# Cached attention decode: most K and V tile loads issued from GpSimd's software DMA queue, a DMA engine's eight rows as one packet

## The chip, the core and the metric

The kernel runs on one core of a Trainium2 chip. The core has TensorE (matrix products), VectorE, ScalarE, GpSimd and SyncE, each with its own instruction stream, and 16 DMA engines that move data between HBM and the on-chip memory SBUF. A DMA is issued from an engine's stream into a queue; the 16 DMA engines work through the queues. The metric is device microseconds of one execution, lower is better; where several runs are told, their median.

## The reference

Two independent sets of inputs, A and B, go through the same attention step with one query token per sequence; the two results stand side by side. Everything is bf16.

```python
def _A_ref(x, k_cache, v_cache, wq, wo):       # B=8, Sq=1, D=1024, H=32, Sk=4096, Dh=128
    q = (x @ wq).reshape(B, Sq, H, Dh).transpose(0, 2, 1, 3)
    scores = einsum("bhqd,bhkd->bhqk", q, k_cache) * (Dh ** -0.5)
    p = softmax(scores, axis=-1)
    o = einsum("bhqk,bhkd->bhqd", p, v_cache)
    return o.transpose(0, 2, 1, 3).reshape(B, Sq, H * Dh) @ wo
```

For each set the K cache and the V cache are 8 x 32 x 4096 x 128 values, and each is read once. Four caches of 268 MB and the weights make the 1107 MB that the profile counts.

## The kernel before

**Tiles.** One tile is eight heads of one sequence: 8 x 4096 x 128 values, 8.39 MB, laid on 128 partitions of 64 KB each, so that each of the 16 DMA engines moves eight rows of 64 KB. There are NQ = 64 K tiles and 64 V tiles (2 sets x 8 sequences x 4 groups of heads), written k0 to k63 and v0 to v63 here. Weights wq and wo of a set are each one tile of the same size. All tiles live in `ring`, three slots of SBUF (line 196): K tiles alternate between slots 0 and 1, V tiles use slot 2 (the last, v63, uses slot 0). A list, `plan` (line 271), has the order of loads: wq A, k0, wq B, k1, v0, k2, v1, k3, v2, and so on, with v63, wo A and wo B last. wo B is cut into four pieces.

**The work on one tile pair n.** A K tile is worked on in four chunks. VectorE multiplies a chunk by the query, broadcast over the partitions (`make_mul`, line 362), and adds its two halves of the head dimension (`make_fold`, line 367). TensorE adds up further by matmuls with an identity (`make_eacc`, line 377), and VectorE reduces the rest (`make_red`, line 385). After four chunks VectorE finds a shift (`make_shift`, lines 391 to 395), ScalarE takes the exponential (line 397), and VectorE spreads the weights over eight columns (`make_pm`, line 402). TensorE multiplies them by the V tile in two halves (`make_pv`, line 414); ScalarE copies the sum (line 422), TensorE extracts (line 431), ScalarE copies out (line 437). The query of the next tile is staged by ScalarE (line 344), broadcast by TensorE (line 349) and copied (line 351).

**The order.** The loop at line 498 writes the instructions of each engine in order. The V part of tile n-1 is put into the chunks of tile n: the shift and the spreading after its first chunk's multiplication, the first half of PV(n-1) in its third chunk, ahead of that chunk's identity matmuls, and the second half in its fourth chunk, ahead of that chunk's. The identity matmuls of a chunk run one chunk ahead of VectorE's reduction of it. After the main passage the last tile is finished, then come the normalisation (`make_norm`) and the projection by wo (`make_proj`, line 467).

**Loads.** `load_tiles` (line 291) issues the loads in the order of `plan`, each as soon as the last user of its slot is known. A K tile's slot is free when the fourth chunk's identity matmuls of its former tenant are done, a V tile's when the second half of PV is. All of these loads are issued from SyncE, by `load_cache` (line 235) for K and V and by `dma` (line 232) for the weights: one hardware queue, served in order. Each waits on a TensorE semaphore first. The small inputs x come from ScalarE's hardware queue at the start. GpSimd has only set-up work at the start (memsets and selects).

**Semaphores and loops.** A DMA into slot w raises the semaphore of key `("t", w)` by 16. The engines' streams are straight code with a loop in the middle: `_repeat` finds that every round waits for the same semaphores with counts that grow evenly. TensorE's loop starts at tile 1, VectorE's and ScalarE's at tile 3 (line 544). SyncE and GpSimd have straight code.

Of the kernel before, what the change touches and what calls it, by code (L numbers as in the profile page):

```python
# [51 lines left out]
class _Program:  # L52
# [13 lines left out]
    def add(self, eng, emit, deps=(), dma_key=None, moves=False):  # L66
        op = _Op(eng, emit, list(deps), dma_key, moves)
        if dma_key is not None:
            self.counts[dma_key] = self.counts.get(dma_key, 0) + 16
            op.token = (dma_key, self.counts[dma_key])  # L70
        for d in op.deps:
            if not (d.eng == "pe" and eng == "pe"):
                d.sig = True
        self.ops[eng].append(op)
        return op
# [89 lines left out]
def _build_kernel(nc, caches, out):  # L165
    B, Sq, D = caches[0][0].shape
    _, H, Sk, Dh = caches[0][1].shape
    NC = len(caches)
# [8 lines left out]
    HB = H // HQ  # L177
    NQ = NC * HB * B
# [3 lines left out]
    MB = HQ * PH  # L182
    NT = 4
    DT = D // NT

    es = ExitStack()
    with es:
# [8 lines left out]
        ring = sb("ring", [128, 3, T * Dh], BF16)  # L196
# [10 lines left out]
        pe = sb("pe", [128, T], BF16)  # L207
# [3 lines left out]
        on_sb = sb("on_sb", [128, NC, B * H + H], BF16)  # L211
        orow = sb("orow", [128, NC, DT], BF16)
        q_sb = PM[:].rearrange("p t j -> p (t j)").rearrange("p (c n) -> p c n", c=NC)
# [8 lines left out]

        wo_cuts = ((0, 20), (20, H - 4), (H - 4, H - 1), (H - 1, H))
        sems = {e: es.enter_context(nc.semaphore(f"c_{e}")) for e in ENGINES[1:]}
        for name, n in (("t", 3), ("w", len(wo_cuts)), ("x", 1), ("out", 1)):
            for i in range(n):
                sems[(name, i)] = es.enter_context(nc.semaphore(f"{name}{i}"))

        P = _Program()
        add = P.add  # L230

        def dma(out_ap, in_ap, key, deps, eng="sp"):
            return add(eng, lambda e: e.dma_start(out_ap, in_ap), deps, dma_key=key)

        def load_cache(to, n, side, key, deps):
            c = where(n)[0]
            size = HQ * Sk * Dh
            whole = caches[c][side].rearrange("b h s d -> (b h s d)")

            def emit(e, at):  # L240
                return e.dma_start(to, whole[bass.ds(at(n % (B * HB) * size, size), size)].rearrange("(p x) -> p x", p=128))
            return add("sp", emit, deps, dma_key=key, moves=True)


        def pool_select(view, base, pattern, dep, op=ALU.not_equal, fill=1.0, step=1):
# [38 lines left out]
        def where(n):  # L284

            return n // (B * HB), n // HB % B, n % HB
# [4 lines left out]
        def load_tiles():  # L291
            while issued[0] < len(plan):
                kind, n, w = plan[issued[0]]
                prev = before[issued[0]]
                dep = opUse.get(prev)
                if prev is not None and dep is None:
                    return
                to, key = ring[:, w, :], ("t", w)
                if kind in ("k", "v"):
                    opT[(kind, n)] = load_cache(to, n, 1 if kind == "k" else 2, key, [dep])  # L300
                elif kind == "wq":
                    opT[(kind, n)] = dma(to[:, 0:DC * H * Dh], caches[n][3].rearrange("(p k) n -> p (k n)", k=DC), key, [dep])
                else:
                    from_ = caches[n][4].rearrange("(p r) n -> p (r n)", r=H)
                    for i, (r0, r1) in enumerate(wo_cuts if n == NC - 1 else ((0, H),)):
                        opT[(kind, n, i)] = dma(to[:, r0 * D:r1 * D], from_[:, r0 * D:r1 * D], key if n < NC - 1 else ("w", i), [dep])
                issued[0] += 1
# [151 lines left out]
        def make_proj(c):  # L459
            w = tile_of("wo", c)  # L460

            for i, (r0, r1) in enumerate(wo_cuts if c == NC - 1 else ((0, H),)):
                def emit(e, r0=r0, r1=r1):
                    for r in range(r0, r1):
                        for q in range(NT):
                            col = r * D + q * DT
                            x = e.matmul(proj[32 * q:32 * (q + 1), 0:DT], on_sb[:, c, r:r + H * B:HQ],  # L467
                                         w[:, col:col + DT], start=(r == 0), stop=(r == H - 1), tile_position=(0, 32 * q))
                    return x
                opProj[c] = add("pe", emit, [opNorm[c], opT[("wo", c, i)], c_pad, opEv.get(c - 1)])  # L470
            if c == NC - 1:
                for engname in P.hinted:
                    add(engname, turn, [opT[("wo", c, len(wo_cuts) - 1)]])
            opEv[c] = add("dve", lambda e: e.tensor_copy(orow[:, c, :], proj[:, 0:DT]), [opProj[c]])  # L474
            outs.append(dma(out[:, 0, c * D:(c + 1) * D].rearrange("b (q n) -> q b n", q=NT), orow[0:128:32 // B, c, :],
# [6 lines left out]
        def emit_xT(e):  # L482
# [5 lines left out]
            return i  # L488
        op_xT = opUse[("x", 0)] = add("pe", emit_xT, [c_ident, op_x[-1]])
        load_tiles()  # L490
        c_xT = add("dve", lambda e: e.tensor_copy(xT[:], misc_bf16[:, 0:NC * DC * B]), [op_xT])
        make_q(0)
# [5 lines left out]
        for n in range(NQ):  # L498
            P.mark(n)
            for r in range(NR):  # L500
                s = n * NR + r
                make_mul(s)
                if s >= LAG:
                    make_red(s - LAG)
                if r == LAG - 1 and n >= 1:
                    make_shift(n - 1)
                fold = make_fold(s)
                if r == LAG - 1 and n >= 1:
                    make_pm(n - 1)
                if n == 0 and r == NR - 1:  # L510
                    for c in range(1, NC):
                        make_q(c)
                        make_qT(c)
                if r == 2 and n >= 1:
                    make_pv(n - 1, 0, RG // 2)
                if r == 3 and n >= 1:
                    make_pv(n - 1, RG // 2, RG)
                    make_acc(n - 1)
                if r == 2 and n + 1 < NQ:
                    make_stage(n + 1)  # L520
                    make_qbc(n + 1)
                make_eacc(s, fold)
                load_tiles()
                if r == 3 and n >= 1:
                    make_ext(n - 1)
        P.mark(NQ)
        n = NQ - 1
# [4 lines left out]
        make_pv(n, 0, RG)  # L532
        make_acc(n)
        load_tiles()
        make_ext(n)
        make_norm(1)
# [4 lines left out]
        counts = P.tokens()  # L541
        for o in op_x:
            o.token = (("x", 0), 16 * NC)
        loops = {"pe": [(1, 2, (NQ - 2) // 2)], "dve": [(3, 2, (NQ - 4) // 2)], "act": [(3, HB, (NQ - 4) // HB)]}

        P.run("sp", nc.sync, sems, part=(0, 2))
        with nc.Block() as block:
# [24 lines left out]
def bass_concat_heads__mha_block_cached__mha_block_cached__decode_kernel(  # L572
    nc, A_x, A_k_cache, A_v_cache, A_wq, A_wo, B_x, B_k_cache, B_v_cache, B_wq, B_wo, out,
):
    caches = [(A_x, A_k_cache, A_v_cache, A_wq, A_wo), (B_x, B_k_cache, B_v_cache, B_wq, B_wo)]
    _build_kernel(nc, caches, out)
# [28 lines left out]
```

## Time and profile before

| | |
|---|---|
| median of 3 runs | 2559.17 us (2559.16 to 2559.21) |
| profiled execution | 2559.26 us |
| its span, first to last instruction | 2558.0 us |
| mean granted TensorE clock | 0.687 |
| read from HBM | 1107.33 MB, 433 GB/s over the span |
| VectorE busy | 2170.2 us |
| TensorE busy | 1117.0 us |

The profile is one execution. Its time is 1.3 us more than its span. A group's line has the source line, the engine, the operation, what it writes and reads, how often, its busy time, the mean time of one in ns, and the idle time just before it with what ended that. A timeline's line has the start and the duration in microseconds, and in brackets the idle time before it and who ended it. `PE` is TensorE, `DVE` VectorE, `ACT` ScalarE, `POOL` GpSimd, `SP` SyncE, and a `q` behind an engine's name is its stream of issues. A queue's line has the number of packets, the MB and the time that its packets took, as a share of the 16 DMA engines' time; q1 is SyncE's hardware queue, q10 ScalarE's, and the kind "instruction" is the loading of code. "DMA packets" counts a tile's row of 64 KB as one packet, and each DMA engine's write of a semaphore as another of 4 bytes.

### The profile page before, as it was taken

How to read it: one execution, taken by the hardware profiler on the slowest of the kernel's cores; microseconds unless marked ns; L12 is line 12 of the kernel's file. 1: busy time of each engine (PE TensorE's matmuls, PEld its weight loads, DVE VectorE, ACT ScalarE, POOL GpSimd, SP SyncE). 2: the span in 40 equal slices, each digit the busy share in tenths (PEclk: the TensorE clock that was granted, in tenths of full speed). 3: DMA queues.
4: the chain of work that ended last, by engine and by line, in shares of the span. 5: the costliest groups of instructions: out<-in, count | busy, mean ns of one | idle time of the engine just before them, and what ended most of it. 6: DMA issues, size and time to landing. Idle time of an engine off the chain costs nothing.

```text
span 2558.0 us, 18889 instructions
## 1 busy us (share of the span) xinstructions
PE 1117.0 (44%) x7712; PEld 396.9 (16%) x7712; DVE 2170.2 (85%) x1042; ACT 129.9 (5%) x401; POOL 2.6 (0%) x15
## 2 busy tenths in 40 slices
PE   2443443443443444444444434444444434434435
PEld 0111111111111111111111111111111111111112
DVE  3898898898898898898898888988988988988983
ACT  1100000000000000000000000000000000000000
POOL 0000000000000000000000000000000000000000
PEclk8666676766767766766666767767767666666667
DMA  9999999999999999999999999999999999999999
GB/s 426 428 440 429 440 429 440 429 438 431 435 433 435 433 432 436 430 439 430 439 430 439 431 439 430 439 430 439 430 438 431 438 431 438 431 436 432 433 436 396
DMA packets 19552, 1107.49 MB, mean 433 GB/s; under 512 B 2184, under 2 KB 2248, under 8 KB 2520
## 3 DMA queue, kind: packets, MB, share of 16 engines
q1 hardware_dynamic: 19512, 1107.34, 99.9%
q8 instruction: 7, 0.11, 0.0%
q10 hardware_dynamic: 32, 0.03, 0.0%
q14 instruction: 1, 0.01, 0.0%
HBM read 1107.33 MB, written 0.03 MB: 433 GB/s over the span
## 4 chain that ended last, share of the span: by engine, by line
DMA 52%; DVE 28%; issue 16%; PE 4%; ACT 0%; another core or an unknown queue 0%; DVEq 0%; SPq 0%
DMA ring<-in_A_k_cache_dram 25%; DMA ring<-in_B_k_cache_dram 25%; DVE ring L362 10%; DVE ring L367 10%; PE red L377 4%; DVE s_sb L385 4%; DVE PM L402 3%; DMA ring<-in_B_wo_dram 2%; DVE rmax L391 1%; DVE rtmp L392 0%; ACT PM L323 0%; PE o L317 0%; DVEq L161 0%; DVE ngm L395 0%
## 5 line engine op out<-in xcount | busy, mean ns | idle before, releaser
L362 DVE TENSOR_TENSOR ring<-ring,qbc 128x8192 bf16<-128x8192 bf16 x256 | 1131.2, 4419 | 306.0 <-DMA ring<-in_A_k_cache_dram 154.9
L377 PE MATMUL red<-ring,ident 128*128 128x512 bf16 x2048 | 782.0, 551 | 1387.8 <-DVE ring L367 1387.8
L367 DVE TENSOR_TENSOR ring<-ring 128x4096 bf16<-128x4096 bf16 x256 | 581.5, 2271 | 0.0
L377 PEld LDWEIGHTS red<-ring,ident 128*128 128x128 bf16 x2048 | 239.3, 128 | 1838.9 <-DVE ring L367 1490.3
L385 DVE TENSOR_REDUCE s_sb<-red 128x64 f32<-128x1024 f32 x256 | 311.2, 1215 | 3.5 <-PE red L377 3.5
L414 PE MATMUL pv<-ring,PM 128*32 128x512 bf16 x4096 | 274.0, 415 | 4.7 <-DVE PM L402 4.7
L402 DVE TENSOR_TENSOR PM<-pe,own_h 128x2048 bf16<-128x2048 bf16 x64 | 146.2, 2284 | 0.7 <-ACT pe L397 0.7
L414 PEld LDWEIGHTS pv<-ring,PM 128*32 128x32 bf16 x4096 | 103.8, 104 | 188.0 <-issue 115.1
L351 ACT ACTIVATE qbc<-misc 128x128 bf16<-128x128 f32 x64 | 17.8, 278 | 1091.7 <-PE misc L349 1091.7
L397 ACT ACTIVATE pe<-s_sb,ngm 128x256 bf16<-128x256 f32 x64 | 32.5, 508 | 465.6 <-DVE ngm L395 465.6
L422 ACT ACTIVATE accS<-pv 128x512 bf16<-128x512 f32 x64 | 38.2, 597 | 352.8 <-PE pv L414 352.8
L431 PEld LDWEIGHTS o<-accS,E 128*32 128x32 bf16 x1024 | 31.2, 100 | 49.4 <-issue 48.2
L431 PE MATMUL o<-accS,E 128*32 128x32 bf16 x1024 | 38.0, 185 | 0.7 <-ACT accS L422 0.7
L437 ACT ACTIVATE o_sb<-o 32x32 f32 (+1 forms) x64 | 11.9, 186 | 449.8 <-PE o L431 441.9
L391 DVE TENSOR_REDUCE rmax<-s_sb 128x1 f32<-128x256 f32 x64 | 26.9, 420 | 2.2
L474 DVE CAST orow<-proj 128x256 bf16<-128x256 f32 x2 | 0.8, 424 | 26.8 <-PE proj L467 26.8
L337 DVE COPY qT<-misc 128x64 bf16<-128x64 bf16 x8 | 3.5, 434 | 18.6 <-PE misc L333 18.6
L344 ACT ACTIVATE qst<-qT 128x128 bf16 (+1 forms) x64 | 18.7, 292 | 1.9 <-DVE qT L337 1.9
L467 PE MATMUL proj<-ring,on_sb 128*32 128x256 bf16 x256 | 11.7, 354 | 16.1 <-DMA ring<-in_A_wo_dram 8.1
L392 DVE TENSOR_SCALAR rtmp<-half,rmax 128x32 f32<-128x32 f32 x64 | 15.4, 241 | 2.3
L395 DVE TRANSPOSE_TENSOR_REDUCE ngm<-rtmp 128x1 f32<-128x32 f32 x64 | 13.5, 211 | 2.2
L349 PE MATMUL misc<-ident,qst 128*128 128x128 bf16 x64 | 14.7, 230 | 0.9 <-ACT qst L344 0.9
(33 smaller groups left out, 65.3 us busy)
## 6 DMA issues: line engine op xcount, KB each, us to landing
ring<-in_B_wo_dram SPq DMA_DIRECT2D x1, 5120.0 KB, 32.9
ring<-in_B_wo_dram SPq DMA_DIRECT2D x1, 2048.0 KB, 37.3
ring<-in_B_wo_dram SPq DMA_DIRECT2D x1, 768.0 KB, 38.7
ring<-in_A_k_cache_dram SPq DMA_DIRECT2D x32, 39.8
ring<-in_A_v_cache_dram SPq DMA_DIRECT2D x32, 27.8
ring<-in_B_k_cache_dram SPq DMA_DIRECT2D x32, 39.7
ring<-in_B_v_cache_dram SPq DMA_DIRECT2D x32, 27.8
ring<-in_B_wo_dram SPq DMA_DIRECT2D x1, 256.0 KB, 38.8
```

The lines of the kernel that those rows point to most:

```text
L344: return e.activation(qst[:, n % 2, :].rearrange("p (j m) -> p j m", m=MP), from_.unsqueeze(2).to_broadcast([128, HQ, MP]), ACTF.Copy)
L351: opQbc[n] = add("act", lambda e: e.activation(qbc[:, n % 2, :], misc[:, 0:Dh], ACTF.Copy), [opQb[n], _at(opMul, NR * (n - 2) + NR - 1)])
L362: opMul[s] = add("dve", lambda e: e.tensor_tensor(v, v, qbc[:, n % 2, :].unsqueeze(1).to_broadcast([128, CT, Dh]), ALU.mult), [opT[("k", n ...
L367: return add("dve", lambda e: e.tensor_tensor(v[:, :, 0:64], v[:, :, 0:64], v[:, :, 64:128], ALU.add), [opMul[s]])
L377: i = e.matmul(dst, ident[:], v[:, g, :, j, :], start=(j == 0), stop=(j == 3))
L385: opRed[s] = add("dve", lambda e: e.tensor_reduce(s_sb[:, n % 2, r * CT:(r + 1) * CT], red_ps[s % 2][:, :].rearrange("p (t w) -> p t w", w ...
L391: m = add("dve", lambda e: e.tensor_reduce(rmax[:], s_sb[:, n % 2, :], AX.X, ALU.max), [opRed[NR * n + NR - 1]])
L397: opExp[n] = add("act", lambda e, at: e.activation(pe[:], s_sb[:, n % 2, :], ACTF.Exp, bias=ngm[:, n % 2:n % 2 + 1], scale=scale, accum_ou ...
L402: opPM[n] = add("dve", lambda e: e.tensor_tensor(PM[:], pe[:].unsqueeze(2).to_broadcast([128, T, HQ]), own_h[:].unsqueeze(1).to_broadcast( ...
L414: i = e.matmul(pv_ps[32 * q:32 * (q + 1), :], PM[:, t:t + 4, :].rearrange("p t j -> p (t j)"), v[:, t * Dh:(t + 4) * Dh], start=(g == 0), ...
L422: opAcc[n] = add("act", lambda e: e.activation(accS[:], pv_ps[:], ACTF.Copy), [opPV[n], _at(opExt, n - 1)])
L431: x = e.matmul(to, E[:, i, PH - 1 - u:PH - 1 - u + MB], accS[:, i * 128 + H * u:i * 128 + H * (u + 1)], start=(i == 0 and u == 0), stop=(i ...
```

## The change

```diff
+    HARD = {"k": 3, "v": 2}
...
-        for name, n in (("t", 3), ("w", len(wo_cuts)), ("x", 1), ("out", 1)):
+        for name, n in (("t", 3), ("g", 3), ("w", len(wo_cuts)), ("x", 1), ("out", 1)):
...
+            soft = key[0] == "g"
 
             def emit(e, at):
-                return e.dma_start(to, whole[bass.ds(at(n % (B * HB) * size, size), size)].rearrange("(p x) -> p x", p=128))
-            return add("sp", emit, deps, dma_key=key, moves=True)
+                from_ = whole[bass.ds(at(n % (B * HB) * size, size), size)].rearrange("(p x) -> p x", p=128)
+                return e.dma_start(to, from_, single_packet=True) if soft else e.dma_start(to, from_)
+            return add("pool" if soft else "sp", emit, deps, dma_key=key, moves=True)
...
-                to, key = ring[:, w, :], ("t", w)
+                to, key = ring[:, w, :], ("t" if n < HARD.get(kind, NC) else "g", w)
...
-        loops = {"pe": [(1, 2, (NQ - 2) // 2)], "dve": [(3, 2, (NQ - 4) // 2)], "act": [(3, HB, (NQ - 4) // HB)]}
+        loops = {"pe": [(3, 2, (NQ - 4) // 2)], "dve": [(3, 2, (NQ - 4) // 2)], "act": [(3, HB, (NQ - 4) // HB)]}
```

K tiles k3 to k63 and V tiles v2 to v63 are issued from GpSimd's stream into its software queue, whose descriptors (the DMA engines' orders) a program on GpSimd writes. The eight rows that a DMA engine moves for such a tile form one packet. The tiles before, and all weights, stay on SyncE's hardware queue. Software loads raise semaphores of their own, `("g", w)`, so that TensorE's waits change with the tiles; its loop starts at tile 3 instead of 1 and runs 30 rounds of two tiles instead of 31. What each load waits for, the slots and the order of `plan` are as before.

## Prediction

> **What bounds the kernel now.** First the page's shares, its queues and the chain of waits, then the transfers of the steady stretch.
>
> ```profile
> PE 1117.0 (44%) x7712; PEld 396.9 (16%) x7712; DVE 2170.2 (85%) x1042; ACT 129.9 (5%) x401; POOL 2.6 (0%) x15
> q1 hardware_dynamic: 19512, 1107.34, 99.9%
> DMA 52%; DVE 28%; issue 16%; PE 4%; ACT 0%; another core or an unknown queue 0%; DVEq 0%; SPq 0%
> ```
>
> One hardware queue carries all the data, and its packets fill the 16 DMA engines for 99.9% of the span. VectorE is the next engine at 85%. So a microsecond in which the engines have nothing to move is a microsecond of the result, and VectorE has some room. The DMA view of the stretch from the first tile's landing to the last K tile's:
>
> ```profile
> DMA packets 18148, 1057.03 MB, mean 434 GB/s; under 512 B 2016, under 2 KB 2016, under 8 KB 2016
> q1 hardware_dynamic: 18144, 1056.97, 100.2%
> q8 instruction: 3, 0.05, 0.0%
> ```
>
> The packets' times add up to 100.2% of the engines' time: they overlap slightly, and no idle time stands between rows. The timeline of VectorE shows when K tiles land (the multiplications that waited for a DMA):
>
> ```profile
> 81.86 4.43 DVE L362 TENSOR_TENSOR ring<-ring,qbc 128x8192 bf16<-128x8192 bf16 x1 [3.07 <-DMA ring<-in_A_k_cache_dram]
> ...
> 120.66 4.42 DVE L362 TENSOR_TENSOR ring<-ring,qbc 128x8192 bf16<-128x8192 bf16 x1 [4.88 <-DMA ring<-in_A_k_cache_dram]
> ...
> 159.39 4.43 DVE L362 TENSOR_TENSOR ring<-ring,qbc 128x8192 bf16<-128x8192 bf16 x1 [4.82 <-DMA ring<-in_A_k_cache_dram]
> ...
> 2477.57 4.42 DVE L362 TENSOR_TENSOR ring<-ring,qbc 128x8192 bf16<-128x8192 bf16 x1 [4.69 <-DMA ring<-in_B_k_cache_dram]
> ```
>
> From tile k1 (81.86) to k63 (2477.57) are 62 periods: 2395.71 / 62 = 38.64 us for a K and a V tile. A tile takes 19.32 us and one of an engine's 16 rows 2.415 us. VectorE idles some 4.8 us in each period. The issues on SP's queue, in order v1, k3, v2, k4, v3:
>
> ```profile
> 111.95 0.33 SPq L241 DMA_DIRECT2D ring<-in_A_v_cache_dram  x1
> 119.32 0.33 SPq L241 DMA_DIRECT2D ring<-in_A_k_cache_dram  x1
> 150.75 0.33 SPq L241 DMA_DIRECT2D ring<-in_A_v_cache_dram  x1
> 158.26 0.33 SPq L241 DMA_DIRECT2D ring<-in_A_k_cache_dram  x1
> 189.48 0.33 SPq L241 DMA_DIRECT2D ring<-in_A_v_cache_dram  x1
> ```
>
> v2 is issued at 150.75, and k3 ahead of it ends at 159.39: its margin is 8.64 us. k4, issued at 158.26, waits for all of v2, which ends at 159.39 + 19.32 = 178.7: a K tile's margin is 20.4 us. Whatever a software issue costs is free up to these margins.
>
> **The change part by part.** 61 K tiles (k3 to k63) and 62 V tiles (v2 to v63) leave SP's queue; wq, k0 to k2, v0, v1 and wo stay.
>
> *The moved issues.* GpSimd's own 15 instructions are its set-up at the start; after that it only waits and issues, in SP's old order and on the same TensorE semaphores. Nothing else stands behind its waits. What a software issue takes until bytes flow is not in the trace. The nearest row from below is SP's first issue, at 0.80 us, with the packets counted up to 1.8 and up to 2.6 us:
>
> ```profile
> 0.80 0.40 SPq L233 DMA_DIRECT2D ring<-in_A_wq_dram  x1
> ...
> DMA packets 0, 0.00 MB, mean 0 GB/s; under 512 B 0, under 2 KB 0, under 8 KB 0
> ...
> DMA packets 16, 1.05 MB, mean 403 GB/s; under 512 B 0, under 2 KB 0, under 8 KB 0
> L590 POOL MEMSET const-uint8-127<- 128x1 uint8 x1 | 0.1, 102 | 0.0
> ```
>
> So at least 1.0 us. From above: if each of the 128 rows cost GpSimd its smallest instruction (102 ns), 13.1 us. I take 2 us, close to SP's row, since writing a descriptor is no whole instruction. In the steady loop 2 us is hidden under 8.64 and costs nothing; without that cover each microsecond above costs 61 us.
>
> A rule speaks against this part: the Trainium skill ("SBUF — State Buffer", the section on who interferes with whom) says that GpSimd can't write descriptors while VectorE is in a mode that uses both port pairs, and that two-input operations take only the read side. By its first half an issue would wait for VectorE to pause; no run here shows it. It gets its own rival below.
>
> *The joining.* Seven packet boundaries in each of 123 tiles go: 861 per engine. The rows that price a boundary are the 4-byte semaphore packets of the x loads (the last row of the fences on the x loads below): 8 packets take 0.2% of 16 engines x 2.5 us, 10 ns each. As packets overlap, the saving lies between 0 and 10 ns, 0 to 8.6 us in all. Below nothing I bound it by a slow period, the one from 81.86 to 120.66: 0.16 us over the mean, x 61 = 9.8 us lost. I take 2 us gained (2.4 ns a boundary): the overlap already hides about 0.2% x 2415 = 4.8 of the 10 ns.
>
> The Trainium skill ("DMA: Bandwidth & Descriptors", why small descriptors are slow) puts a packet's fixed cost at about 3 cycles, beside one cycle for each 32 B, and calls joining worthwhile only for descriptors up to 256 B. Beside the 2048 cycles of a 64 KB row that is 0.15%; by it the gain would be an estimated 3 us (61 x 38.64 x 0.15% x 7/8), and the sum 2566.
>
> *The hand-over from SP's queue to GpSimd's.* This is the largest term. In one queue k3 stands behind v1. In two, the engines choose. The trace has one place with two filled queues: the x loads on ACT's queue beside wq and k0 on SP's. Issues and landing, then the x queue's packets in 7 to 9.5 us (the rows of one x) and in 9.5 to 12 us (their semaphores); the next two stretches of 2.5 us read the same for the other x:
>
> ```profile
> 2.49 0.59 ACTq L233 DMA_DIRECT2D ring<-in_A_x_dram  x1
> 3.12 0.28 ACTq L233 DMA_DIRECT2D ring<-in_B_x_dram  x1
> ...
> 15.87 1.11 PE L486 MATMUL misc<-ident,ring 8*128 8x8 bf16 x16 [15.87 <-DMA ring<-in_B_x_dram]
> ...
> 43.27 4.42 DVE L362 TENSOR_TENSOR ring<-ring,qbc 128x8192 bf16<-128x8192 bf16 x1 [9.76 <-DMA ring<-in_A_k_cache_dram]
> ```
>
> ```profile
> q10 hardware_dynamic: 8, 0.02, 1.7%
> ...
> q10 hardware_dynamic: 8, 0.00, 0.2%
> ```
>
> x landed by 15.87, not after k0 at 43.27: one small packet went in after each 2.4 us row of the other queue. Engines take turns packet by packet. Now a packet of k3 holds eight rows and a packet of v1 one. k2 lands at 120.66, and v1's rows begin. k3, issued at 119.32 + 2, goes in after a row or two of v1, whole. Both tiles together are done when they were before, 120.66 + 38.64 = 159.3; but v1, which landed near 140.0, is now the last of the two. (The Trainium skill, "DMA: Bandwidth & Descriptors", on queues and rings, says that an engine drains a whole packet before it switches; of joined packets no run here shows it, and without it v1 lands one row earlier, a rival below.) TensorE's rows that need v1 and what stands behind them on TensorE:
>
> ```profile
> 142.82 1.93 PE L414 MATMUL pv<-ring,PM 128*32 128x512 bf16 x32
> 144.68 0.23 PE L349 MATMUL misc<-ident,qst 128*128 128x128 bf16 x1
> 146.96 1.90 PE L377 MATMUL red<-ring,ident 128*128 128x512 bf16 x8 [2.05 <-DVE ring L367]
> 148.79 1.91 PE L414 MATMUL pv<-ring,PM 128*32 128x512 bf16 x32
> 154.63 3.60 PE L377 MATMUL red<-ring,ident 128*128 128x512 bf16 x8 [3.93 <-DVE ring L367]
> ...
> 181.55 3.03 PE L414 MATMUL pv<-ring,PM 128*32 128x512 bf16 x32
> ```
>
> The first half of PV(1), at 142.82 before, starts at 159.3. Behind it stand the query broadcast (0.23), the third chunk's fold sums (line 377) and the second half; only then is v2 issued. That is 1.93 + 0.2 + 1.90 + 1.91 = 5.9 us with these fast rows, 3.03 + 0.2 + 3.60 + 3.03 = 9.9 with the slow ones; I take 7.5. With 2 us for the issue, v2's bytes start at 168.8, and the engines idle from 159.3: **9.5 us lost**, between 5.9 + 1.0 = 6.9 and 9.9 + 13.1 = 23. It is lost once: VectorE resumes with the third chunk's sums near 164, k4 is issued by about 171, well before v2 ends at 188; k3's multiplication starts near 168, v3 is issued 30.1 us later (159.39 to 189.48 before), at 198, and k4 ends at 168.8 + 38.6 = 207. The margins are back, and nothing is regained, as the engines are full until the end.
>
> *The hand-back, v63 to wo,* costs nothing: wo of A is issued at 2507.66, when v63 has been on the engines since about 2477.57 + 19.3 = 2497. Even row by row in turns, v63 would land 8.5 us late, near 2525, and PV(63), 6.2 us, and its tail of some 2 us end before the projection starts:
>
> ```profile
> 2507.66 0.33 SPq L233 DMA_DIRECT2D ring<-in_A_wo_dram  x1
> ...
> 2520.21 6.18 PE L414 MATMUL pv<-ring,PM 128*32 128x512 bf16 x64 [4.67 <-DVE PM L402]
> ...
> 2535.82 5.26 PE L467 MATMUL proj<-ring,on_sb 128*32 128x256 bf16 x128 [8.10 <-DMA ring<-in_A_wo_dram]
> ```
>
> *TensorE's loop* starts two tiles later, so two tiles more of straight code are fetched (the instruction queue q8 above has three packets in the whole stretch). TensorE, 44% busy, covers that; a fetch may stand behind one joined packet, 19.3 us at worst, if it isn't made ahead of need.
>
> *Sum.* The profiled execution took 2559.26 us (span 2558.0 and 1.3 around it), 0.1 over the median of the runs: 2559.3 + 9.5 - 2 = **2567 us**.
>
> **The rivals.**
>
> *No collision (not slower).* Place: the same hand-over. v1 lands early enough if its rows go first, by a preference for SP's queue or because the first software issue is late. To be hidden, v2 must be issued by 159.3 - 2, so v1 must land by 149.8: no more than four rows of k3 ahead of it (4 x 2.415 = 9.7 after 140.0). Then 2559.3 - 2 = 2557; 2551 with 10 ns a boundary. The x loads speak against a preference.
>
> *Joining is worth more.* At 11 ns a boundary (9.5 / 861) the hand-over is paid back; at 25 ns, 21 us, the time is 2547. The 10 ns packets speak against it.
>
> *Row by row.* If joining does not hold the rows together, v1 lands at 159.3 - 2.4 = 156.9, the loss is 7.1 and the gain nothing: 2566.
>
> *Descriptors come too late.* If GpSimd is held up by VectorE or needs the 13.1 us, each V tile is 4.5 us past its margin: 61 x 4.5 = 272, with the hand-over some 2840. VectorE's 4.8 us pause in each period, right before the K tile lands, speaks against it: a blocked write would get through there.
>
> *The software stream is slower.* The slowest full slice of the page has 428 GB/s against a mean of 434, 1.4%: 61 x 38.64 x 1.4% = 33, in all 2600.
>
> ```profile
> GB/s 426 428 440 429 440 429 440 429 438 431 435 433 435 433 432 436 430 439 430 439 430 439 431 439 430 439 430 439 430 438 431 438 431 438 431 436 432 433 436 396
> ```
>
> **How the numbers follow.** Forecast 0.50 (its own range 2562 to 2574), no collision 0.18, joining worth more 0.06, row by row 0.08, late descriptors 0.08, slower stream 0.10. The range, 2553 to 2588, holds the forecast, row by row, most of no collision and the milder part of a slower stream. 0.2%, 5.1 us, is about what a measurement of this kernel can tell from no change. Faster than 2554.1: 0.12, from joining and the best of no collision. Slower than 2564.3: 0.66, from the forecast above its lower end, row by row, late descriptors and a slower stream. Between: 0.22.
>
> **What would show it.** Right: after k2's landing PV(1) waits about 16 us for v1; the GB/s near 160 us drop for some 10 us, once; afterwards the K landings are 38.60 to 38.64 us apart, and joined packets make the mean packet eight times as large. Wrong: PV(1) starts near 143; or the periods differ from 38.64 by over 0.1 us, which is 6 us in all; or VectorE's idle time waits for V tiles in every period.

## The result and the profile after

The changed kernel takes 2569.72 us (median of six runs, 2568.45 to 2570.51), the kernel before 2559.16 us (2559.01 to 2559.21) beside it: a ratio of 1.0041, with a 95% interval of 1.0028 to 1.0054. It is 10.6 us slower; 2567 us with a range of 2553 to 2588 had been forecast. The profiled execution took 2569.77 us, its span 2568.5 us.

The page of the changed kernel: shares, the GB/s of 40 slices of 64 us, and the data queues.

```profile
PE 1122.1 (44%) x7712; PEld 398.9 (16%) x7712; DVE 2170.2 (84%) x1042; ACT 129.9 (5%) x401; POOL 67.7 (3%) x138
...
GB/s 424 433 368 426 439 428 440 439 427 439 427 441 435 431 439 427 440 431 436 439 427 439 432 436 438 428 439 428 440 438 428 439 427 441 435 431 439 427 440 394
...
q0 software_dynamic: 17712, 1031.81, 92.7%
q1 hardware_dynamic: 1800, 75.53, 6.8%
```

93% of the bytes went over to the software queue. One slice is low, the third (128 to 193 us): 368 GB/s where the kernel before had 440 there. The others before the last lie between 424 and 441, as they did (426 to 440). The packet counts say that a row of 64 KB is still recorded as a packet of its own: 123 tiles x (128 rows + 16 semaphore writes) = 17712. The K tiles' landings, by VectorE's timeline of the changed kernel (k4, k5 and k63):

```profile
208.02 4.43 DVE L365 TENSOR_TENSOR ring<-ring,qbc 128x8192 bf16<-128x8192 bf16 x1 [7.53 <-DMA ring<-in_A_k_cache_dram]
246.81 4.42 DVE L365 TENSOR_TENSOR ring<-ring,qbc 128x8192 bf16<-128x8192 bf16 x1 [4.88 <-DMA ring<-in_A_k_cache_dram]
...
2487.82 4.42 DVE L365 TENSOR_TENSOR ring<-ring,qbc 128x8192 bf16<-128x8192 bf16 x1 [4.65 <-DMA ring<-in_B_k_cache_dram]
```

and of the kernel before, k4 and k5:

```profile
197.98 4.43 DVE L362 TENSOR_TENSOR ring<-ring,qbc 128x8192 bf16<-128x8192 bf16 x1 [4.67 <-DMA ring<-in_A_k_cache_dram]
...
236.59 4.42 DVE L362 TENSOR_TENSOR ring<-ring,qbc 128x8192 bf16<-128x8192 bf16 x1 [4.71 <-DMA ring<-in_A_k_cache_dram]
```

k4 lands 10.0 us late, k63 10.25 us late (2487.82 against 2477.57). From k5 to k63 are 58 periods: 2241.01 us after, 2240.98 us before. So the steady stream is as fast as it was, and the loss is there by k5 (10.22 us; 10.04 of it by k4). The rows of TensorE at that place, changed kernel:

```profile
156.88 3.61 PE L417 MATMUL pv<-ring,PM 128*32 128x512 bf16 x32 [13.97 <-DMA ring<-in_A_v_cache_dram]
160.41 0.29 PE L352 MATMUL misc<-ident,qst 128*128 128x128 bf16 x1
160.49 2.71 PE L380 MATMUL red<-ring,ident 128*128 128x512 bf16 x8
163.13 1.91 PE L417 MATMUL pv<-ring,PM 128*32 128x512 bf16 x32
```

PV(1), at 142.82 before, waits 14 us for v1 and starts at 156.88. GpSimd's own issues of k3, v2 and k4:

```profile
119.73 0.69 POOL L244 DMA_DIRECT2D ring<-in_A_k_cache_dram  x1 [115.57 <-PE red L380]
165.37 0.53 POOL L244 DMA_DIRECT2D ring<-in_A_v_cache_dram  x1 [44.95 <-PE pv L417]
168.92 0.53 POOL L244 DMA_DIRECT2D ring<-in_A_k_cache_dram  x1 [3.02 <-PE red L380]
```

v2 is issued at 165.37 instead of 150.75. The DMA view of short stretches of the changed kernel: two of 2.4 us from 123.4 us on, then 158.9 to 166.5 us, then 166.5 to 170 us.

```profile
q1 hardware_dynamic: 9, 0.59, 56.7%
q0 software_dynamic: 7, 0.46, 44.1%
...
q0 software_dynamic: 9, 0.59, 56.7%
q1 hardware_dynamic: 7, 0.46, 44.1%
...
DMA packets 0, 0.00 MB, mean 0 GB/s; under 512 B 0, under 2 KB 0, under 8 KB 0
...
q0 software_dynamic: 25, 1.64, 128.5%
```

The first four rows are the collision: in each 2.4 us, the time of one row, the 16 engines start 9 rows of one queue and 7 of the other, and in the next 2.4 us it is the other way about. The engines take turns row by row, although the rows were to be joined. (The packet records, put in a chain where one packet ends and the next begins, alternate strictly on all 16 engines until v1 is through, here and in e1 below.) The fifth row is the price: 7.6 us without a single packet. The last is v2's start.

### The profile page after: what moved, and what is told of

The parts are those of the page before. It is cut to its first block, busy times and chain, and to the rows that moved or that the text cites. A ratio compares the mean times of both kernels' runs of the same rounds, so it can differ in the third digit from the quotient of the medians.

```text
span 2568.5 us, 18873 instructions
## 1 busy us (share of the span) xinstructions
PE 1122.1 (44%) x7712; PEld 398.9 (16%) x7712; DVE 2170.2 (84%) x1042; ACT 129.9 (5%) x401; POOL 67.7 (3%) x138
## 4 chain that ended last, share of the span: by engine, by line
DMA 51%; DVE 28%; issue 16%; PE 5%; ACT 0%; another core or an unknown queue 0%; SPq 0%; DVEq 0%
DMA ring<-in_B_k_cache_dram 25%; DMA ring<-in_A_k_cache_dram 23%; DVE ring L365 10%; DVE ring L370 10%; PE red L380 4%; DVE s_sb L388 4%; DVE PM L405 3%; DMA ring<-in_A_v_cache_dram 2%; DMA ring<-in_B_wo_dram 1%; DVE rmax L394 1%; DVE rtmp L395 0%; PE pv L417 0%; ACT PM L326 0%; SPq L234 0%
## 5 line engine op out<-in xcount | busy, mean ns | idle before, releaser
L244 POOL DMA_DIRECT2D ring<-in_B_v_cache_dram x32 | 16.9, 528 | 969.8 <-PE pv L417 929.6
L244 POOL DMA_DIRECT2D ring<-in_A_v_cache_dram x30 | 15.8, 528 | 942.3 <-PE pv L417 942.3
L244 POOL DMA_DIRECT2D ring<-in_A_k_cache_dram x29 | 15.5, 533 | 297.8 <-PE red L380 297.8
L244 POOL DMA_DIRECT2D ring<-in_B_k_cache_dram x32 | 16.9, 528 | 208.4 <-PE red L380 208.4
## 6 DMA issues: line engine op xcount, KB each, us to landing
ring<-in_B_v_cache_dram POOLq DMA_DIRECT2D x32, 27.5
ring<-in_A_v_cache_dram POOLq DMA_DIRECT2D x30, 27.5
```

What stands on the lines that cost most here:

```text
L244: return e.dma_start(to, from_, single_packet=True) if soft else e.dma_start(to, from_)
```

## The experiments

Times are medians; beside each, on the same chip, ran the kernel before (medians 2559.07 to 2559.12 us). Each edit is made to the changed kernel.

| run | edit | us, lowest to highest |
|---|---|---|
| changed kernel | none | 2569.72, 2568.45 to 2570.51 |
| e1 | rows not joined | 2568.84, 2568.52 to 2570.30 |
| e2 | k3 issued later | 2560.40, 2560.17 to 2560.73 |
| e3 | v1 from the software queue too | 2561.59, 2560.74 to 2562.03 |
| e4 | all K and V from the hardware queue | 2560.54, 2560.27 to 2560.61 |
| e5 | V from the software queue, K not | 3085.18, 3079.48 to 3090.87 |
| e6 | k3 issued a little later | 2564.16, 2563.55 to 2564.68 |
| e7 | e4, TensorE's loop from tile 5 | 2560.44, 2560.24 to 2561.01 |
| e8 | k2 and v1 from the software queue too | 2569.23, 2568.51 to 2569.82 |
| e9 | e2 with rows not joined | 2560.50, 2560.09 to 2560.84 |

**e1, joining alone.**

```diff
-                return e.dma_start(to, from_, single_packet=True) if soft else e.dma_start(to, from_)
+                return e.dma_start(to, from_)
```

> The changed kernel with the joining taken out: the software loads leave out the one-packet flag, all else as in the change. Theory (the whole loss is the hand-over, joining is worth nothing): the trace of the changed kernel has v1 landing at 156.9 and K periods of 38.64, as row by row; so this should take the same 2569.7, within 1.5 us, with v1 landing near 157 again. Rival 'joining gains something that the hand-over hides' (2 us or more): 2572 or more, with K periods above 38.66. Rival 'joining costs': below 2568.

2568.84 us, within the changed kernel's spread, and v1 is waited for as long (14.12 us against 13.97). TensorE's row in e1:

```profile
157.09 3.61 PE L417 MATMUL pv<-ring,PM 128*32 128x512 bf16 x32 [14.12 <-DMA ring<-in_A_v_cache_dram]
```

With the flag PV(1) starts at 156.88, without it at 157.09. The flag does not hold a tile's rows together against another queue.

**e2, the hand-over without the collision.** `late` is the first chunk's identity matmuls of tile k2; k3's issue waits for it too.

```diff
+                late = opEacc.get(2 * NR) if (kind, n) == ("k", 3) else None
+                if (kind, n) == ("k", 3) and late is None:
+                    return
...
-                    opT[(kind, n)] = load_cache(to, n, 1 if kind == "k" else 2, key, [dep])
+                    opT[(kind, n)] = load_cache(to, n, 1 if kind == "k" else 2, key, [dep, late])
```

> The change, but k3's software issue waits in addition for the first chunk's identity matmuls of tile k2 (near 133 us in both traces), so that most of v1's rows are through before k3's bytes come. Theory: v1 lands by 145 instead of 156.9, v2 is issued by 153, the engines never idle, and the time is that of the kernel before, 2559 to 2561. Rival 'GpSimd's queue itself is slower or its first use costs the 10 us': 2567 to 2571 as in the change.

2560.40 us: 9.3 us of the 10.6 are gone, although all 123 tiles still come from GpSimd. The rows of e2, GpSimd's issues of k3 and v2, TensorE's PV(1), and k63's landing:

```profile
132.97 0.69 POOL L244 DMA_DIRECT2D ring<-in_A_k_cache_dram  x1 [128.83 <-PE red L383]
152.59 0.53 POOL L244 DMA_DIRECT2D ring<-in_A_v_cache_dram  x1 [18.93 <-PE pv L420]
...
144.98 2.88 PE L420 MATMUL pv<-ring,PM 128*32 128x512 bf16 x32 [2.27 <-DMA ring<-in_A_v_cache_dram]
...
2477.63 4.43 DVE L368 TENSOR_TENSOR ring<-ring,qbc 128x8192 bf16<-128x8192 bf16 x1 [4.67 <-DMA ring<-in_B_k_cache_dram]
```

v1 lands by 145, as expected, v2 is issued some seven microseconds before k3 is through (159.54), and k63 lands where it did before the change (2477.57). The first use of GpSimd's queue costs nothing. The last 1.3 us stand behind k63 (e4).

**e6, in between.** The same edit with `late = opMul.get(2 * NR)`, VectorE's first multiplication of k2.

> As e2_k3_later, but k3's software issue waits for VectorE's first multiplication of k2 (its end near 125 us), between the change's 119.7 and e2's 133. Theory: about three of v1's rows go unhindered, each of the other rows waits one row of k3, v1 lands near 150 to 152, v2 is issued near 158 to 160, and the engines idle 1 to 4 us: 2561 to 2565, between e2's 2560.4 and the change's 2569.7. Rival 'the 9 us come or do not come, by whether k3 is ahead of v1's start': 2560.4 or 2569.7.

2564.16 us. Its rows, k3's issue and PV(1):

```profile
125.77 0.69 POOL L244 DMA_DIRECT2D ring<-in_A_k_cache_dram  x1 [121.64 <-DVE ring L368]
...
152.09 3.60 PE L420 MATMUL pv<-ring,PM 128*32 128x512 bf16 x32 [9.14 <-DMA ring<-in_A_v_cache_dram]
```

The issue of k3 at 119.7, 125.8 and 133.0 us makes PV(1) start at 156.9, 152.1 and 145.0, and the time 2569.7, 2564.2 and 2560.4. The loss follows v1's landing and is no all-or-nothing.

**e3, another boundary.** The software queue takes over with a V tile: v1 (issued near 112) meets the last rows of k2.

```diff
-    HARD = {"k": 3, "v": 2}
+    HARD = {"k": 3, "v": 1}
```

> The software queue takes over one tile earlier: v1 is its first tile, k2 the hardware queue's last. Theory: at the hand-over v1's rows (issued near 112) then take turns with the last three or four rows of k2. k2 lands 2 to 9 us late, near 123 to 130, and TensorE's margin for v2 swallows it: 2559 to 2564. By a row-by-row count on one DMA engine, with the delays of the traces put in, nothing is lost. Rival 'any hand-over between the queues costs about 10 us': 2567 to 2571.

2561.59 us, 1.2 above e2. k2's landing in e3:

```profile
125.64 4.42 DVE L365 TENSOR_TENSOR ring<-ring,qbc 128x8192 bf16<-128x8192 bf16 x1 [9.51 <-DMA ring<-in_A_k_cache_dram]
```

k2 lands 5 us late, and more than half of that is swallowed by v2's margin: v2 is issued 3.4 us later than in e2 (156.00), and k4 lands 2.1 us later (200.21 against 198.12). The expectation's count, by which nothing is lost, was missed by that. A hand-over is not dear as such; it depends on which tile is passed and what waits for it.

**e8, the same collision earlier.** `HARD = {"k": 2, "v": 1}`.

> The hand-over two tiles earlier: k2 is the first software tile (issued near 82, when v0, issued near 74, has not begun), v0 the hardware queue's last V tile. Theory: the same collision as in the change one pair earlier: v0 lands near 116 to 118 instead of 101, PV(0) waits for it some 12 us, and the engines idle once for 6 to 9 us: 2566 to 2570. Rival 'earlier tiles have room to take the delay, as in e3': 2559 to 2562.

2569.23 us. In e8 it is PV(0) that waits (14.5 us, some 12 had been expected), and the loss is that of the changed kernel:

```profile
118.31 3.60 PE L417 MATMUL pv<-ring,PM 128*32 128x512 bf16 x32 [14.52 <-DMA ring<-in_A_v_cache_dram]
```

**e5, the collision in every period.** `HARD = {"k": 64, "v": 2}`: K from the hardware queue throughout, V from the software queue.

> K tiles all stay on SyncE's hardware queue, V tiles from v2 come from GpSimd's: the two queues are both filled in every period, not once. Theory (the engines take turns row by row, and a V tile that shares with a K tile lands a whole tile late): every period loses what the change loses once. A row-by-row count gives some 8 us per period, about 500 us in all, 3000 to 3110; v3, v4 and later PV products wait for their V tile in every period. Rival 'the loss belongs to the switch from one queue to the other, not to sharing': 2567 to 2575.

3085.18 us, a ratio of 1.2055 (1.2033 to 1.2077): 526 us, or 8.6 us for each of the 61 periods from v2's on. The group of PV matmuls in e5, with its idle time and what ended it:

```profile
L417 PE MATMUL pv<-ring,PM 128*32 128x512 bf16 x4096 | 346.9, 499 | 937.3 <-DMA ring<-in_B_v_cache_dram 478.9 <-DMA ring<-in_A_v_cache_dram 458.4
```

and the GB/s of 40 slices of 2.4 us over two of its periods (1002 to 1098 us):

```profile
GB/s 355 0 0 0 437 410 437 410 437 437 437 437 437 382 437 437 437 437 437 437 109 0 0 0 437 437 437 437 437 437 437 437 437 437 437 437 437 437 437 410
```

Full rate while there is work, and a hole of three slices in each period: TensorE waits for the late V tile (937 us in all, 5 before the change), only then frees its slot, and the engines have nothing to do meanwhile.

**e4, TensorE's loop alone.** All loads stay on SyncE's queue; what is left of the change is TensorE's loop from tile 3.

```diff
-    HARD = {"k": 3, "v": 2}
+    HARD = {"k": 64, "v": 64}
```

> The change with every K and V load left on SyncE's hardware queue: only TensorE's loop from tile 3 and the unused semaphores differ from the kernel before. Theory: 2559.2 within 1 us. Rival 'the longer straight code of TensorE costs part of the 10 us through code loading': 2561 or more.

2560.54 us: 1.4 above the kernel before, outside both spreads, and the theory's bound of 1 us is missed. k63 lands at 2477.63 in e4 too. What comes later are the last 16 projection matmuls, in the kernel before and then in e4:

```profile
2554.55 0.98 PE L467 MATMUL proj<-ring,on_sb 128*32 128x256 bf16 x16 [0.72 <-DMA ring<-in_B_wo_dram]
```

```profile
2555.89 1.08 PE L470 MATMUL proj<-ring,on_sb 128*32 128x256 bf16 x16 [2.20 <-DMA ring<-in_B_wo_dram]
```

They wait for the last rows of wo and start 1.34 us later. In e4 the DMA view of 2553 to 2555 us has a code packet beside the data, which the kernel before has earlier, in 2550 to 2552.7 us, and no later one. The second row here is that view for 2554.7 to 2556.1 us of e4; in the kernel before no packet starts between 2554.81 and 2555.8 us:

```profile
q8 instruction: 1, 0.02, 3.0%
...
q1 hardware_dynamic: 12, 0.03, 5.4%
```

A code packet of 16 KB holds an engine for 0.96 us (3.0% of 16 engines x 2 us). The 12 packets at the end take 1.2 us in all (5.4% of 16 engines x 1.4 us), one behind the other: a single engine is still at work. The records name no engine, but the row just ahead of these 12 begins at 2554.28, as the code packet ends (2554.29), and every other packet that ends about then has a successor of its own. So the code packet stood in front of the last rows of wo. That is read from one trace; no run moved the packet alone.

**e7, more of the same.** e4 with `"pe": [(5, 2, (NQ - 6) // 2)]`.

> e4_all_hard with TensorE's loop starting at tile 5 and running 29 rounds. In e4 the last 16 projection matmuls start 1.3 us later than in the kernel before, and a code packet of 16 KB is on a DMA engine 1.5 us later than the last one of the kernel before. Theory (where the code's pages fall decides whether the last page comes in front of the last wo rows): the tail changes with the code's length, not step by step: 2559.0 to 2560.7. Rival 'each two tiles of straight code cost 1.4 us': 2562.

2560.44 us: no second step of 1.4 us, as the theory had it. Nor is the first step gone, although e7's code packets fall at other times.

**e9, joining without the collision's blur.** e2 without the flag.

> e2_k3_later without the one-packet flag: joining alone, with no idle time at the hand-over to blur it (e2's runs lie within 0.6 us). Theory (joining changes nothing, as turns are taken row by row with it and the periods stay 38.64): 2560.4 within 0.4 us. My prediction's term (2 us gained by joining): 2562.4. Rival 'joining costs' (e1 came out 0.9 us below the change): 2559.5.

2560.50 us against e2's 2560.40: the flag is worth nothing that can be measured here, in either direction.

## Why the prediction came out, step by step

The direction, the place and most of the mechanism held: one collision at the hand-over, v1 the tile that suffers, idle DMA engines while TensorE catches up, nothing regained. What did not hold is how the engines share (row by row) and what joining is worth. The sum had a net loss of 7.5 us (9.5 - 2); 10.6 were measured. Two terms were too large by some 3.2 us together (v1's landing 2.4, the software issue 0.8), and 6.3 us were missing elsewhere (TensorE's catching up 1.0, the restart 2.0, joining 2.0, TensorE's loop 1.3). That 2567 came so near is in part luck: the errors cancelled by half.

- *A joined packet goes in whole.* Wrong. I had v1 land at 159.3, after all of k3; it took turns with k3's rows, and PV(1) began at 156.88, where the rival "row by row" had it (156.9). This alone shortens the loss by 2.4 us. The Trainium skill ("DMA: Bandwidth & Descriptors", the section on queues, rings and completion order) has an engine drain a whole packet before it switches; here rows of 64 KB alternated with the one-packet flag (the changed kernel) and without it (e1). Whether the flag forms one packet that is interrupted, or none, these records cannot tell.
- *TensorE's catching up,* taken as 7.5 us, took 8.5 (156.88 to 165.37), as the first PV ran at 3.61 us. *The software issue,* taken as 2 us, took 1.2 (165.37 to 166.6). By these rows the hand-over should cost 166.6 - 159.3 = 7.3 us; e2 says 9.3, by medians, and k4 lands 10.0 us late in the profiled execution.
- *The restart after the idle time* was no term of the sum, and it cost some 2 us: from v2's first bytes to k4's landing pass 41.4 us instead of 38.6 and a few tenths for landing. The DMA view of the changed kernel shows two parts of it, in 166.5 to 167.5, 179.4 to 179.5 and 206.5 to 207.43 us:

```profile
q0 software_dynamic: 16, 1.05, 313.2%
...
q8 instruction: 1, 0.02, 55.1%
...
q0 software_dynamic: 2, 0.07, 16.3%
```

  The 16 first rows of v2 took 3.13 us each (313.2% of 16 engines x 1 us, over 16), 0.7 more than a row of the stream. And a code packet of 0.88 us held one engine at 179.44. At k4's end one engine alone is late: from 206.5 on only its semaphore write, at 207.42, and its next row are left, while the other 15 are through by 206.43. Followed back from packet to packet, it is the engine that had the code packet. The kernel before has no code packet between 133 and 623 us; e4, with the changed loop, has one at 181.66, and there k63 lands as before (2477.63). So a part of these 2 us may belong to the longer straight code, met by engines that had just started together; no run separates the two.
- *Joining, 2 us gained.* Wrong: nothing (e9), and 2241.01 against 2240.98 us over 58 periods. The range from 0 to 8.6 us held, at its lower end. Either the rows, which overlap already (100.2%), leave no gap to save, or the flag joined nothing; the records can't tell. The estimate of 3 us by the page of the Trainium skill is not borne out.
- *TensorE's loop, costed at nothing.* Wrong in the place: it costs nothing in the steady stretch (k63 lands at 2477.63 in e4), but a code packet also takes a DMA engine's time, the tail has no cover for that, and the different code costs 1.4 us there (e4). In the changed kernel's profiled execution the part behind k63 is only 0.25 us longer (80.68 against 80.43 us of span), so the 10.6 us split into 9.3 + 1.3 by medians and 10.25 + 0.25 in the trace. The split is known to about 1 us.
- *The hand-back, v63 to wo,* costed at nothing. Right: e2 has it and e4 has not, and they take 2560.40 and 2560.54 us.
- *Margins of the steady loop.* Right. The issues from v3 on hide under their margin of 8.64 us, and the periods are unchanged.
- *Late descriptors, slower stream.* They did not happen. The Trainium skill ("SBUF — State Buffer", who interferes with whom) warns that VectorE can keep GpSimd from writing descriptors; here a software V tile landed a median 27.5 us after its issue, 27.8 before from the hardware queue, with VectorE 84% busy. This kernel's long VectorE rows are two-input operations, which the page itself expects to leave descriptor writing alone. The DMA issues of the changed kernel's page:

```profile
ring<-in_B_v_cache_dram POOLq DMA_DIRECT2D x32, 27.5
```

- *What would show it.* Three of the marks held (the wait for v1, 14 us where about 16 were given; the one dip in GB/s; periods of 38.64 us). The fourth, packets eight times as large, did not come: the records list rows either way.

No version here is faster than the kernel before. e2 is the change without its collision, and it is the plain loop change of e4 in time.

## What to carry to other kernels

Before moving loads to a second queue, look for the moments at which both queues are filled, and ask which tile is passed there, how late it lands if each of its rows waits for one of the other's, and who then holds a slot. One such moment cost 9 us here, one in each period 526 us, and the order of issue within one queue had given the right priority for nothing. In this stream, with rows of 64 KB and no gaps between them, the flag had nothing left to give.

## What the runs showed of the hardware

- The engines alternate between a hardware and a software queue one 64 KB row at a time, with the one-packet flag set or not (9 and 7 rows, then 7 and 9, in successive 2.4 us; PV(1) from 156.88 and 157.09 us).
- A software issue of 128 rows of 64 KB took GpSimd 0.53 us and its first bytes moved about 1.2 us after its start (165.37 to 166.6), near the hardware queue's 1.0 us.
- Loaded code competes with data for the DMA engines: a packet of 16 KB takes nearly 1 us of one engine, and a change to code alone moved the end by 1.4 us (e4). In the changed kernel the engine that had one finished k4 a microsecond after the other 15 (207.42 against 206.43).
- After an idle stretch the first rows of 64 KB took 3.13 us each instead of 2.42 (software queue, changed kernel, from 166.5); the first rows of the kernel before, from the hardware queue, took as long (3.13 us, from 1.8).
